# Attention and a low-rank mixer MLP on one core: the mixer by rows of tokens, turned by DMA, with a new order of score blocks and a new pacing

## The chip, the core and the metric

The kernel runs on one NeuronCore of a Trainium2 chip. Its engines run at the same time, each through its own instruction queue in order: TensorE (PE in the profile, PEld its weight loads), VectorE (DVE), ScalarE (ACT), GpSimd (POOL) and SyncE (SP), which here only issues DMA transfers. The kernel's matmuls write to PSUM; the other operands lie in SBUF, 128 partitions wide. Engines wait for each other by semaphores.

The metric is the device time of one execution in microseconds. The time before is 633.39 us, the median of three runs (633.01 to 634.63). A profile is one more execution, recorded by the hardware.

## The reference

Attention over 8 batches, 12 heads, 448 tokens and 64 dimensions a head, with q and k normalised by their root mean square; its result, laid side by side over the heads, is x (448 tokens x 768). A mixer adds a low-rank mix over tokens to x, which gives u, and a two-layer MLP follows.

```python
q_n, k_n = rmsnorm(q, g_q), rmsnorm(k, g_k)
attn = softmax(1.0 / np.sqrt(D) * q_n @ k_n.T)      # per batch and head
x = attn @ v                                        # heads side by side: 448 x 768
h = x.T @ U @ V                                     # U: 448 x 32, V: 32 x 448
u = x + h.T
ch = np.maximum(u @ w_ch1, 0.0) @ w_ch2             # 768 -> 3072 -> 768
out = u + ch
```

## The kernel before

*Tiles.* PE computes in bf16. 448 tokens are three windows of 128 columns and a remainder of 64 (`NJ = 3`, `R = 64`). Weights `w1b` and `w2b` stay in SBUF. `uT` (768 rows as 6 blocks of 128 partitions, 512 columns) holds u turned, with dimensions on the partitions; `hT` holds the hidden layer, 24 blocks of 128 rows. Even batches use columns 64 to 511 of both, odd batches 0 to 447, so that the last 64 tokens of an even batch and the last 64 of the following odd one lie side by side, in columns 448 to 511 and 384 to 447, and go through the second layer as one window of 128.

*Attention* (list `att`) goes by pairs of heads (`pr`, six a batch, 48 in all); two pairs make a group (`gi`, 24 in all) whose q, k and v are loaded and normalised together. For a pair there are four `Sc`: matmuls of kz by qT, 128x448 each, two in blocks 0 to 2 (a double block) and one in block 3, and behind each an exp on ACT into `E` (L333). `sc` has two buffers, so PE can be two blocks ahead of ACT. Two `V` then multiply `E` by v and the ones beside it, 14 matmuls each, and DVE divides (L352, L353) and writes `x`, which is laid out by rows of tokens.

*A block of norms* prepares a group: `squares` on ACT, `sums` on DVE, then `scale_all` (rs on ACT, L130 and L131; the scalings and the copies of v on POOL), then the turn of q and k. For the first six groups (`DMA_FROM = 6`) the turn is done by PE (`T`, `turn`); from then on by `turn_dma`: four DMA transposes on SP (L301, L303), and right behind them in the same queue `load`, six transfers for the group two further on (L88, L95, L99). SP also issues the output (L422).

*The mixer and MLP* (list `mlp`) goes by batches. `mix_t` multiplies x by U (24 small matmuls, L366), `mix_tr` turns the small result (L373). `mix` then makes one block of 128 dimensions of `uT`: a matmul of the turned product by V (L381, 448 columns), and four matmuls by an identity that turn x and add it in the same PSUM bank (L383, L384); DVE copies the bank to `uT` (L385). Six `mix` make a batch. `up` (24 a batch) is six matmuls of 448 columns, each reading all tokens of the batch from `uT`, and a relu on ACT. `down` goes by windows of 128 tokens and halves of 384 output dimensions, in four quarters of six matmuls (L404); the last quarter adds u with three identity matmuls that read `uT` (L410), DVE copies the bank to `ob` (L415) and, after the second half, two transfers take it out.

*PSUM.* `sc` has a pool of two buffers of its own (`ps_sc`). All other tiles (pv, ph, po, pt, pu, pw) share the four buffers of the pool `ps`, a bank each.

*The order of the work* is written out by hand. Before the first mixer, the six pairs of batch 0 run alone. Then a planner takes from `att` and `mlp` in turn, by the costs written beside each piece: the next attention piece is taken as long as attention's share done is not above the MLP's share, where the MLP's total is lessened by `LEAD` = 1.9 batches, so that attention is through before the MLP. Within `att`, a pair's order is Sc 0, V half 0 of the pair before, Sc 1, Sc 2, V half 1, Sc 3; the norms of the next group stand behind Sc 1 of every first pair of a group.

## Time and profile before

| | |
|---|---|
| median of three runs | 633.39 us |
| profiled execution, its own time | 632.76 us |
| its span, first to last instruction | 631.0 us |
| mean granted clock of TensorE | 0.993 |
| busy PE, ACT, DVE, POOL | 599.9, 317.3, 197.0, 139.2 us |
| MLP matmuls L391 and L404, busy | 239.5 and 240.5 us |
| first `mix_t` | at 47.77 us |
| end of the last matmul | about 626 us |

A line of the profile names the source line, the engine, the operation, the tiles written and read (`out<-in`), the shapes and how often; then busy time, mean time of one in ns, and the engine's idle time just before it with what ended it. A "q" behind an engine's name is its instruction queue, where DMA transfers are issued. PE's durations overlap, since matmuls are pipelined; what one costs is read from start to start.

### The profile page before, as it was taken

How to read it: one execution, taken by the hardware profiler on the slowest of the kernel's cores; microseconds unless marked ns; L12 is line 12 of the kernel's file. 1: busy time of each engine (PE TensorE's matmuls, PEld its weight loads, DVE VectorE, ACT ScalarE, POOL GpSimd, SP SyncE). 2: the span in 40 equal slices, each digit the busy share in tenths (PEclk: the TensorE clock that was granted, in tenths of full speed). 3: DMA queues.
4: the chain of work that ended last, by engine and by line, in shares of the span. 5: the costliest groups of instructions: out<-in, count | busy, mean ns of one | idle time of the engine just before them, and what ended most of it. 6: DMA issues, size and time to landing. Idle time of an engine off the chain costs nothing.

```text
span 631.0 us, 11686 instructions
## 1 busy us (share of the span) xinstructions
PE 599.9 (95%) x4880; PEld 363.2 (58%) x4880; DVE 197.0 (31%) x459; ACT 317.3 (50%) x483; POOL 139.2 (22%) x255
## 2 busy tenths in 40 slices
PE   3769999899999999989999999999999999999996
PEld 1545566555666556655566655665566655665564
DVE  7675233521334223242133422333223330130011
ACT  5785753377544674347644477337853344004300
POOL 4682203303302321330330332033033000000000
PEclk9989999999999999989999999999999999999999
DMA  9999944454366336526445623654425110120022
GB/s 260 243 240 238 239 100 88 119 133 97 66 153 148 84 89 151 124 68 125 109 79 153 155 46 95 150 118 92 107 45 79 42 26 1 25 51 1 1 51 50
DMA packets 95012, 66.88 MB, mean 106 GB/s; under 512 B 60528, under 2 KB 91376, under 8 KB 94960
## 3 DMA queue, kind: packets, MB, share of 16 engines
q1 hardware_dynamic: 88112, 56.22, 38.0%
q0 software_dynamic: 6576, 9.47, 8.2%
q8 instruction: 38, 0.62, 0.4%
q10 hardware_dynamic: 272, 0.46, 0.2%
q14 instruction: 14, 0.11, 0.1%
HBM read 52.19 MB, written 11.01 MB: 100 GB/s over the span
## 4 chain that ended last, share of the span: by engine, by line
PE 88%; DVE 5%; ACT 3%; issue 2%; POOL 1%; DMA 1%; POOLq 0%; DVEq 0%
PE po L404 35%; PE ph L391 34%; PE sc L332 9%; PE pv L349 5%; DVE uT L385 3%; ACT E L333 2%; PE po L410 1%; PE pv L345 1%; DVE ssq L124 1%; PE pt L282 1%; DMA qf<-in_q_dram 1%; ACT sq L121 1%; PE pu L366 1%; POOL kp L134 1%; PE ph L381 0%
## 5 line engine op out<-in xcount | busy, mean ns | idle before, releaser
L333 ACT ACTIVATE E<-sc,gg 128x896 bf16<-128x896 f32 x192 | 172.7, 910 | 140.7 <-PE sc L332 140.2
L391 PE MATMUL ph<-uT,w1b 128*128 128x448 bf16 x1152 | 239.5, 354 | 3.3 <-DVE uT L385 3.0
L404 PE MATMUL po<-w2b,hT 128*128 128x384 bf16 x1344 | 240.5, 326 | 0.0
L404 PEld LDWEIGHTS <-hT 128*128 128x128 bf16 x1344 | 127.7, 98 | 82.2
L391 PEld LDWEIGHTS <-w1b 128*128 128x128 bf16 x1152 | 110.0, 98 | 101.1 <-issue 5.7
L393 ACT ACTIVATE hT<-ph 128x448 bf16<-128x448 f32 x192 | 103.5, 544 | 126.6 <-PE ph L391 124.2
L332 PE MATMUL sc<-qT,kz 128*128 128x448 bf16 x336 | 95.9, 364 | 9.1 <-ACT E L333 8.3
L152 POOL TENSOR_TENSOR qn<-qf,rs 128x384 bf16<-128x384 f32 x36 | 29.9, 831 | 305.2 <-ACT rs L131 305.2
L415 DVE COPY ob<-po 128x384 f32<-128x384 f32 x56 | 31.2, 558 | 165.0 <-PE po L410 162.3
L352 DVE RECIPROCAL r<-pv 128x4 f32<-128x4 f32 x96 | 17.5, 182 | 207.8 <-PE pv L349 207.7
L349 PE MATMUL pv<-va,E 128*128 128x65 bf16 x1152 | 59.0, 196 | 0.8 <-ACT E L333 0.8
L349 PEld LDWEIGHTS <-E 128*128 128x128 bf16 x1152 | 52.2, 99 | 8.1 <-issue 1.1
L332 PEld LDWEIGHTS <-kz 128*128 128x128 bf16 x336 | 31.0, 99 | 33.1 <-issue 13.5
L124 DVE TENSOR_REDUCE ssq<-sq 128x14 f32<-128x896 f32 x48 | 49.7, 1076 | 1.1 <-ACT sq L121 1.1
L345 PE MATMUL pv<-vl,E 128*128 128x130 bf16 x192 | 42.9, 223 | 0.0
L353 DVE TENSOR_TENSOR x<-pv,r 128x256 bf16<-128x256 f32 x96 | 40.8, 424 | 3.3
L152 POOL TENSOR_TENSOR kp<-kf,rs 128x384 bf16<-128x384 f32 x36 | 29.9, 829 | 0.0
L385 DVE CAST uT<-ph 128x448 bf16<-128x448 f32 x48 | 26.6, 616 | 0.9 <-PE ph L384 0.7
L121 ACT ACTIVATE sq<-qf 128x896 f32<-128x896 f32 x24 | 22.6, 942 | 2.9 <-DMA qf<-in_q_dram 2.9
L345 PEld LDWEIGHTS <-E 128*128 128x128 bf16 x192 | 19.1, 99 | 7.1 <-issue 0.9
L121 ACT ACTIVATE sq<-kf 128x896 f32<-128x896 f32 x24 | 22.6, 940 | 0.0
L160 POOL CAST va<-vf 128x768 bf16<-128x768 f32 x24 | 20.4, 850 | 0.1
(67 smaller groups left out, 248.7 us busy)
## 6 DMA issues: line engine op xcount, KB each, us to landing
qf<-in_q_dram SPq DMA_DIRECT2D x24, 448.0 KB, 4.3
out_dram<-ob SPq DMA_DIRECT2D x56, 192.0 KB, 2.8
kf<-in_k_dram SPq DMA_DIRECT2D x23, 448.0 KB, 5.4
vf<-in_v_dram SPq DMA_DIRECT2D x48, 192.0 KB, 5.6
w1b<-in_moe_w_ch_dram POOLq DMA_DIRECT2D x4, 1152.0 KB, 20.9
w2b<-in_moe_w_ch_dram POOLq DMA_DIRECT2D x4, 1152.0 KB, 32.4
vf<-in_v_dram SPq DMA_DIRECT2D x48, 32.0 KB, 5.1
qT<-qn SPq DMA_TRANSPOSE x36, 3.0
```

The costliest lines, as they stand in the source:

```text
L121: nc.scalar.activation(sq, staged[gi][i], AF.Square)
L124: nc.vector.tensor_reduce(ssqs[gi][:, i, :], sqs.pop((gi, i)), AX, ALU.add)
L152: nc.gpsimd.tensor_tensor(main.rearrange("p (t i) d -> p i t d", i=2), src[:, c, :2 * NJ].rearrange("p (i t) d -> p i t d", i=2), rs[:, c, ...
L332: nc.tensor.matmul(sc[:, i, :S], kz[:, c:c + P], qT, start=True, stop=True)
L333: nc.scalar.activation(es[(b, pr)][:, 2 * r:2 * r + n, :], sc[:, :n, :S], AF.Exp, scale=scal, bias=bias)
L345: nc.tensor.matmul(pv[:, i].rearrange("p e d -> p (e d)"), E[:, NJ, w:w + P], vl[:, lp, :], start=True, stop=False)
L349: nc.tensor.matmul(pv[:, i, e, :], E[:, e * (NJ + 1) + j, w:w + P], va[:, (lp + 2 * e) * NJ + j, :], start=False, stop=(e == 1 and j == NJ ...
L353: nc.vector.tensor_tensor(xs[b].rearrange("p i (h d) -> p i h d", d=D)[:, 2 * half:2 * half + 2, h0:h0 + 3:2, :], pv[:, :, :, :D], r.rearr ...
L385: nc.vector.tensor_copy(uT[:, dt, off:off + S], ph)
L391: nc.tensor.matmul(ph, w1b[:, dt, ht * P:(ht + 1) * P], uT[:, dt, off:off + S], start=(dt == 0), stop=(dt == KD - 1))
L393: nc.scalar.activation(hT[:, ht, off:off + S], ph, AF.Relu)
L404: nc.tensor.matmul(po, hT[:, ht, col:col + P], w2b[:, ht, half * HALF:(half + 1) * HALF], start=(ht == 0), stop=False)
```

## The change

1. *Mixer by rows.* From batch 1 on (`ROWS_FROM = 1`) `mix` is gone. `mix_rows` works on one window of 128 tokens and 384 dimensions: three matmuls with V's columns as weights, and DVE adds the result to x in place (for the last 64 tokens, into a tile `u_rest`). After the second half one DMA transpose on SP takes the window into `uT`: 28 of them, four a batch, three of 128x768 and one of 64x768. Batch 0 keeps `mix` for `uT` and runs `mix_rows` between its `up`s, for the output alone.
2. *The output.* `down` has no identity matmuls; DVE adds u (from the x tile or `u_rest`) to the bank in place of the copy.
3. *Where it stands.* `mix_t`, `mix_tr` and the eight `mix_rows` of the next batch stand among the last 14 quarters of `down` of the batch before (`PRE = 14`); the last `mix_rows` has five quarters behind it.
4. *Tokens of odd batches* are ordered so that their remainder comes first (`WIN`, `POS_ODD`, the scaling before the turn), and U and V have a second form of their last window: one more transfer to `Ub`, 64 more columns in `Vm`.
5. *Attention's order.* Sc 0, Sc 1, V half 0 of the pair before, Sc 2, Sc 3, V half 1. Norms stand behind Sc 2 (behind Sc 1 for the very first pair). A batch's last two `V` stand together, ahead of the next batch's first block.
6. *Pacing.* `LEAD` is 1.8, and a function `due` spreads batch 1's attention over what the MLP does before `mix_t` of batch 1, and the rest over the rest.
7. *Buffers.* Three for x (two before), two for `ob` (three before). The small tiles of the gains live in an `ob` buffer. `prep_v` (the copies of V on POOL) moves from behind T of group 2 to behind the scaling of group 1.

```diff
-LEAD = 1.9
+ROWS_FROM = 1
+LEAD = 1.8
...
-    WIN = [0, P, 2 * P, S - P]
+    WIN = [[0, P, 2 * P, S - P], [R, R + P, R + 2 * P, 0]]
...
-    xp = ctx.enter_context(tc.tile_pool(name="xp", bufs=2))
-    outp = ctx.enter_context(tc.tile_pool(name="outp", bufs=3))
+    xp = ctx.enter_context(tc.tile_pool(name="xp", bufs=3))
+    outp = ctx.enter_context(tc.tile_pool(name="outp", bufs=2))
...
+    nc.gpsimd.dma_start(Ub[0:R, NJ + 1, :], Urows[:, 2 * NJ, :])
...
+    POS_ODD = [x + 1 for x in POS[:2 * NJ]] + [0]
...
+    u_rest = consts.tile([P, dm], BF16)
+
+    def urows(b, col, half):
+        h = slice(half * HALF, (half + 1) * HALF)
+        return u_rest[:, h] if col == SM else xs[b][:, (col - (0 if b % 2 else R)) // P, h]
+
+    def mix_rows(b, w, half):
+
+        odd = b % 2
+        off = 0 if odd else 64
+        h = slice(half * HALF, (half + 1) * HALF)
+        ph = ps.tile([P, HALF], FP32, name="pm", tag="ps")
+        vc = w * P if w < NJ else (SM if odd else S - P)
+        for i in range(HALF // P):
+            dt = half * (HALF // P) + i
+            nc.tensor.matmul(ph[:, i * P:(i + 1) * P], Vm[:, dt % NQ, vc:vc + P], tTs[b][:, dt // NQ, :],
+                             start=True, stop=True)
+        x = xs[b][:, w, h]
+        lo, hi = (0, P) if w < NJ else (0, R) if odd else (R, P)
+        dst = x if w < NJ else u_rest[lo:hi, h]
+        nc.vector.tensor_tensor(dst, ph[lo:hi], x[lo:hi], ALU.add)
+        if half == 1 and b >= ROWS_FROM:
+            full = xs[b][:, w, :] if w < NJ else u_rest[lo:hi, :]
+            c = off + w * P
+            nc.sync.dma_start_transpose(uT[:, :, c:c + hi - lo], full)
...
-        nd = HALF // P
-        for i in range(nd):
-            nc.tensor.matmul(po[:, i * P:(i + 1) * P], uT[:, half * nd + i, col:col + P], ident,
-                             start=False, stop=(i == nd - 1))
...
-        nc.vector.tensor_copy(ob[:, half * HALF:(half + 1) * HALF], po)
+        nc.vector.tensor_tensor(ob[:, half * HALF:(half + 1) * HALF], po, urows(b, col, half), ALU.add)
...
+    def norms(gi):
+        add_att(0.0, scale_all, gi)
+        if gi >= DMA_FROM:
+            add_att(0.0, turn_dma, gi)
+        if gi + 2 < len(groups):
+            add_att(0.0, load, gi + 2)
...
+        if pr == 0 and i > 0:
+            add_att(0.55, V, *pairs[i - 1], 0)
+            add_att(0.55, V, *pairs[i - 1], 1)
         add_att(0.38, Sc, b, pr, 0)
-        if i > 0:
-            add_att(0.55, V, *pairs[i - 1], 0)
...
         add_att(0.38, Sc, b, pr, 1)
...
+        if pr != 0:
+            add_att(0.55, V, *pairs[i - 1], 0)
...
+        if i == 0:
+            norms(gi + 1)
+        add_att(0.38, Sc, b, pr, 2)
+        if i > 0 and a == 0 and more:
+            norms(gi + 1)
...
+        add_att(0.19, Sc, b, pr, 3)
+        if pr != 0:
+            add_att(0.55, V, *pairs[i - 1], 1)
...
+    PRE = 14
...
+            if b < ROWS_FROM and ht % 2 == 0 and ht < 4 * NW:
+                mlp.append((0.17, mix_rows, (b, ht // 4, ht // 2 % 2), b))
...
+        if ROWS_FROM <= nb < B:
+            pre[n - PRE] = [(0.77, mix_t, (nb,), nb)]
+            pre[n - PRE + 1] = [(0.11, mix_tr, (nb,), nb)]
+            for w in range(NW):
+                for half in range(2):
+                    pre[n - PRE + 2 + 2 * w + half] = [(0.17, mix_rows, (nb, w, half), nb)]
...
+    m_end = m_all * (1.0 - LEAD / B)
+
+    def due(c):
+
+        if c < m_one:
+            return a_one * c / m_one
+        return a_one + (a_all - a_one) * (c - m_one) / (m_end - m_one)
+
...
-        take_att = ia < len(att) and (not may_mlp or ca / a_rest <= cm / m_rest)
+        take_att = ia < len(att) and (not may_mlp or ca <= due(cm))
...
-            if f is T and a == (2, 0):
-                prep_v()
+                if a == (1,):
+                    prep_v()
```

More of the change, by code (lines that the diff above doesn't have):

```diff
@@ L47 @@
     R = S - SM
-    WIN = [0, P, 2 * P, S - P]
-    NW = len(WIN)
+    WIN = [[0, P, 2 * P, S - P], [R, R + P, R + 2 * P, 0]]
+    NW = len(WIN[0])
     D1 = D + 1
@@ L147, in scale_dma @@
                 dst = normed[gi][0][:, :, c]
-                main, rest = dst[:, :2 * NJ], dst[:, 2 * NJ]
+                odd = groups[gi][0] % 2
+                main, rest = dst[:, odd:odd + 2 * NJ], dst[:, (1 - odd) * 2 * NJ]
             else:
@@ L189 @@
     make_identity(nc, ident)
-    grow = consts.tile([1, 2, D], FP32)
+    small = outp.tile([P, dm], FP32, name="ob", tag="ob")
+    grow = small[0:1, 0:2 * D].rearrange("o (i d) -> o i d", i=2)
     for i, g in enumerate((g_q, g_k)):
@@ L206 @@
     bias = gg[:, 1:2]
-    gp = consts.tile([1, 2 * D + 1], FP32)
-    ones = consts.tile([1, P], FP32)
+    gp = small[0:1, 2 * D:4 * D + 1]
+    ones = small[0:1, 4 * D + 1:4 * D + 1 + P]
     nc.vector.memset(ones, 1.0)
@@ L243, in load_w2 @@
         )
-    Ub = consts.tile([P, NW, rank], BF16)
-    nc.vector.memset(Ub[:, NJ, :], 0.0)
+    Ub = consts.tile([P, NJ + 2, rank], BF16)
+    nc.vector.memset(Ub[:, NJ:, :], 0.0)
     Urows = moe_U.rearrange("(p j) r -> p j r", j=NT)
@@ L251 @@
     nc.gpsimd.dma_start(Ub[R:P, NJ, :], Urows[:, 2 * NJ, :])
+    nc.gpsimd.dma_start(Ub[0:R, NJ + 1, :], Urows[:, 2 * NJ, :])
     NQ = P // rank
     Vf = outp.tile([P, dm], FP32, name="ob", tag="ob")[:, :S]
-    Vm = consts.tile([P, NQ, S], BF16)
+    Vm = consts.tile([P, NQ, S + R], BF16)
     for m in range(NQ):
@@ L265, in prep_v @@
                                   cols[:, :2 * NJ].rearrange("r (i t) p -> r i t p", i=2))
-            nc.gpsimd.tensor_copy(Vm[r, m, SM:], cols[:, 2 * NJ])
+            nc.gpsimd.tensor_copy(Vm[r, m, SM:S], cols[:, 2 * NJ])
     tb_bufs = [consts.tile([P, 2 * P], BF16, name=f"tb{i}") for i in range(2)]
@@ L280, in turn @@
         pt = pts[(gi, i)] = ps.tile([P, NT, 2, R], BF16, name="pt", tag="ps")
+        pos = POS_ODD if i == 0 and groups[gi][0] % 2 else POS
         for j in range(NT):
-            nc.tensor.transpose(pt[:, POS[j]].rearrange("p a r -> p (a r)"),
+            nc.tensor.transpose(pt[:, pos[j]].rearrange("p a r -> p (a r)"),
                                 normed[gi][i][:, j].rearrange("p c d -> p (c d)"), ident)
@@ L343, in V @@
         for i in range(2):
-            w = WIN[2 * half + i]
+            w = WIN[b % 2][2 * half + i]
             nc.tensor.matmul(pv[:, i].rearrange("p e d -> p (e d)"), E[:, NJ, w:w + P], vl[:, lp, :],
@@ L365, in mix_t @@
             for j in range(NW):
-                nc.tensor.matmul(pt[:, dt, :], xs[b][:, j, dt * P:(dt + 1) * P], Ub[:, j, :],
+                nc.tensor.matmul(pt[:, dt, :], xs[b][:, j, dt * P:(dt + 1) * P], Ub[:, j if j < NJ else NJ + b % 2, :],
                                  start=(j == 0), stop=(j == NW - 1))
@@ L380, in mix @@
         xb = xs[b][:, :, dt * P:(dt + 1) * P]
-        nc.tensor.matmul(ph, tTs[b][:, dt // NQ, :], Vm[:, dt % NQ, :], start=True, stop=False)
+        nc.tensor.matmul(ph, tTs[b][:, dt // NQ, :], Vm[:, dt % NQ, :S], start=True, stop=False)
         for j in range(NJ):
@@ L404, in down @@
             nc.tensor.matmul(po, hT[:, ht, col:col + P], w2b[:, ht, half * HALF:(half + 1) * HALF],
-                             start=(ht == 0), stop=False)
+                             start=(ht == 0), stop=(ht == KH - 1))
         if part < nparts - 1:
             return
-        nd = HALF // P
-        for i in range(nd):
-            nc.tensor.matmul(po[:, i * P:(i + 1) * P], uT[:, half * nd + i, col:col + P], ident,
-                             start=False, stop=(i == nd - 1))
         if half == 0:
@@ L434 @@
         more = gi + 1 < len(groups)
+        if pr == 0 and i > 0:
+            add_att(0.55, V, *pairs[i - 1], 0)
+            add_att(0.55, V, *pairs[i - 1], 1)
         add_att(0.38, Sc, b, pr, 0)
-        if i > 0:
-            add_att(0.55, V, *pairs[i - 1], 0)
-        if a == 1 and more:
-            add_att(0.39 if gi + 1 < DMA_FROM else 0.0, T, gi + 1, 0)
         if a == 0 and i > 0 and more:
@@ L443 @@
         add_att(0.38, Sc, b, pr, 1)
-        if a == 0 and more:
-            add_att(0.0, scale_all, gi + 1)
-            if gi + 1 >= DMA_FROM:
-                add_att(0.0, turn_dma, gi + 1)
-            if gi + 3 < len(groups):
-                add_att(0.0, load, gi + 3)
+        if pr != 0:
+            add_att(0.55, V, *pairs[i - 1], 0)
+        if a == 1 and more:
+            add_att(0.39 if gi + 1 < DMA_FROM else 0.0, T, gi + 1, 0)
+        if i == 0:
[3 more added lines that the diff above has]
+            norms(gi + 1)
         if a == 1 and more:
             add_att(0.39 if gi + 1 < DMA_FROM else 0.0, T, gi + 1, 1)
-        add_att(0.38, Sc, b, pr, 2)
-        if i > 0:
+        add_att(0.19, Sc, b, pr, 3)
+        if pr != 0:
             add_att(0.55, V, *pairs[i - 1], 1)
-        add_att(0.19, Sc, b, pr, 3)
         if a == 1 and gi + 2 < len(groups):
@@ L466 @@
             done_at[a[0]] = n + 1
+    PRE = 14
     mlp = []
     for b in range(B):
-        if b == 0:
-            mlp.append((0.77, mix_t, (b,), b))
-            mlp.append((0.11, mix_tr, (b,), b))
-        for dt in range(KD):
-            mlp.append((0.39, mix, (b, dt), b))
+        if b < ROWS_FROM:
+            if b == 0:
+                mlp.append((0.77, mix_t, (b,), b))
+                mlp.append((0.11, mix_tr, (b,), b))
+            for dt in range(KD):
+                mlp.append((0.39, mix, (b, dt), b))
         for ht in range(KH):
             mlp.append((1.14, up, (b, ht), b))
+            if b < ROWS_FROM and ht % 2 == 0 and ht < 4 * NW:
+                mlp.append((0.17, mix_rows, (b, ht // 4, ht // 2 % 2), b))
         cols = (64, 192, 320) if b % 2 == 0 else (384, 0, 128, 256)
-        for col in cols:
+        n = len(cols) * 8
+        nb = b + 1
+        pre = {}
+        if ROWS_FROM <= nb < B:
[4 more added lines that the diff above has]
+                    pre[n - PRE + 2 + 2 * w + half] = [(0.17, mix_rows, (nb, w, half), nb)]
+        for c, col in enumerate(cols):
             for half in range(2):
                 for part in range(4):
-                    last = col == cols[-1] and half == 1
-                    if b + 1 < B and last and part == 1:
-                        mlp.append((0.77, mix_t, (b + 1,), b + 1))
-                    if b + 1 < B and last and part == 3:
-                        mlp.append((0.11, mix_tr, (b + 1,), b + 1))
-                    mlp.append((0.98 + (0.17 if part == 3 else 0.0), down, (b, col, half, part, 4), b))
+                    mlp.extend(pre.get(c * 8 + half * 4 + part, []))
+                    mlp.append((0.98, down, (b, col, half, part, 4), b))
     todo = [(load_w1, (c, 4)) for c in range(4)] + [(load_w2, (c, 4)) for c in range(4)]
@@ L519 @@
     a_from = done_at[0]
-    a_rest = sum(c for c, _, _ in att[a_from:])
-    m_batch = sum(m[0] for m in mlp if m[3] == 0)
-    m_rest = sum(m[0] for m in mlp) - LEAD * m_batch
+    a_all = sum(c for c, _, _ in att[a_from:])
+    a_one = sum(c for c, _, _ in att[a_from:done_at[1]])
+    m_all = sum(m[0] for m in mlp)
+    m_one = 0.0
+    for m in mlp:
+        if m[3] > 0:
+            break
+        m_one += m[0]
+    m_end = m_all * (1.0 - LEAD / B)
[3 more added lines that the diff above has]
+        return a_one + (a_all - a_one) * (c - m_one) / (m_end - m_one)
     while ia < len(att) or im < len(mlp):
         may_mlp = im < len(mlp) and ia >= done_at[mlp[im][3]]
-        take_att = ia < len(att) and (not may_mlp or ca / a_rest <= cm / m_rest)
+        take_att = ia < len(att) and (not may_mlp or ca <= due(cm))
         if take_att:
```

## The prediction, made before the changed kernel ran

> **What bounds the kernel now.** I read the page first: busy shares, the chain that ended last, the groups. Then the PE timeline for the price of each piece, the waits for where PE stands still, and the queue of SP, because the change puts new transfers into it.

> ```profile
> PE 599.9 (95%) x4880; PEld 363.2 (58%) x4880; DVE 197.0 (31%) x459; ACT 317.3 (50%) x483; POOL 139.2 (22%) x255
> PE 88%; DVE 5%; ACT 3%; issue 2%; POOL 1%; DMA 1%; POOLq 0%; DVEq 0%
> L385 DVE CAST uT<-ph 128x448 bf16<-128x448 f32 x48 | 26.6, 616 | 0.9 <-PE ph L384 0.7
> qT<-qn SPq DMA_TRANSPOSE x36, 3.0
> kz<-kp SPq DMA_TRANSPOSE x36, 3.5
> ```

> PE is the bound: 88% of the chain. A microsecond of matmul removed, or of PE idle added, is a microsecond of span. The last two rows price a transfer of the kind that the change adds: issue to landing 3.0 us (448 packets of 256 B) and 3.5 us (896).

> PE timeline, start and duration, two pieces of `mix` and the end of the last `down`:

> ```profile
> 121.96 0.35 PE L381 MATMUL ph<-Vm,tT 128*128 128x448 bf16 x1
> ...
> 122.34 0.35 PE L381 MATMUL ph<-Vm,tT 128*128 128x448 bf16 x1
> ...
> 621.57 0.33 PE L410 MATMUL po<-ident,uT 128*128 128x128 bf16 x3
> ...
> 621.74 4.06 PE L404 MATMUL po<-w2b,hT 128*128 128x384 bf16 x24
> 625.64 0.33 PE L410 MATMUL po<-ident,uT 128*128 128x128 bf16 x3
> ```

> One `mix` costs PE 0.385 us (start to start), three 128x128 matmuls 0.17, a quarter of a `down` 0.976 (621.74 to 625.64, by 4), an `up` 1.14, a double score block 0.38, a single one 0.19, a `V` 0.50.

> The queue of SP around one block of norms (four turns of q and k, six loads), and the copy whose output transfer stands behind it in program order:

> ```profile
> 120.94 1.25 SPq L301 DMA_TRANSPOSE qT<-qn  x1
> 123.02 1.24 SPq L303 DMA_TRANSPOSE kz<-kp  x1
> 124.35 1.58 SPq L301 DMA_TRANSPOSE qT<-qn  x1
> 125.98 1.30 SPq L303 DMA_TRANSPOSE kz<-kp  x1
> 127.37 0.91 SPq L88 DMA_DIRECT2D qf<-in_q_dram  x1
> 128.38 0.43 SPq L88 DMA_DIRECT2D kf<-in_k_dram  x1
> 128.86 1.39 SPq L95 DMA_DIRECT2D vf<-in_v_dram  x2
> 130.30 1.95 SPq L99 DMA_DIRECT2D vf<-in_v_dram  x2
> 132.35 1.19 SPq L422 DMA_DIRECT2D out_dram<-ob  x2
> ```

> ```profile
> 122.16 0.56 DVE L415 COPY ob<-po 128x384 f32<-128x384 f32 x1 [0.85 <-PE po L410]
> ```

> `ob` was ready at 122.72, its transfer was issued at 132.35. SP goes in order, so whatever stands behind a block waits for all of it, 9.6 us here. Nobody needs an output soon, so before the change this costs nothing. That row decides my forecast.

> **The change, part by part** (profiled execution: span 631.0, own time 632.76, 0.63 under the median of 633.39).

> *Removed from PE.* 42 `mix` (batches 1 to 7) x 0.385 = 16.2. Identity matmuls of 56 `down` x 0.17 = 9.5. *Added:* 64 `mix_rows`, three 128x128 matmuls each, the form of L410: 64 x 0.17 = 10.9. Net -14.8.

> *The wait for uT at a batch's start.* The waits give PE 3.0 us in 7 waits on uT plus 5.7 us of PEld "issue" at L391. From batch 1 on, the gaps in the PE timeline there, beyond a matmul's 0.19, come to 0.55, 2.4, 0.25, 0.6 and 0.65, and the clock fell to half behind the second (below, 1.7): 6.1 in all. I take -5.5 and leave 0.6 for the handover at the clean starts.

> *The start, to 47.77 us (the first `mix_t`).* ACT sets it. Two double blocks first keep ACT fed past `V` and `T`: ACT waited 8.0 us for scores between 9 and 53 us. The four Vm casts (POOL 33.5 to 38.1, which held the third scaling back to 38.16 although its rs ended at 36.97) move to POOL's idle time 22.2 to 27.1. The first mixer no longer has three score blocks and a pair of squares ahead of it. I worked the ACT chain through by rows (0.91 a double block, 0.6 a single, 1.7 the squares) and get the first `mix_t` near 43.3, with 0.9 us less PE work done. Gain 0 to 4.5; I take 3, below the 3.6, as the weights land no earlier.

> *At nothing:* DVE gets 64 adds and loses 42 casts (0.55 each): about +10 us on an engine 31% busy; uncovered, only the last add, under 0.1. One more Ub transfer, 0.54 us on POOL, ahead of a 2.0 us wait. Windows, POS_ODD and WIN: same instructions. Third x buffer: it only lets `V` run further ahead. Two `ob` buffers for three: 0 to +3, taken 0; an output has twelve quarters, some 12 us and the attention between them, until its buffer is wanted, and needs a block's hold to miss that (rival B). LEAD and the pacing change which matmuls follow which, not their number; in the planner's list no batch's attention has to be forced ahead of a waiting mixer, the tightest being `mix_t` of batch 1, one quarter (0.976) behind its last `V`, whose reciprocal and multiply take 0.6.

> Without lateness: 632.8 - 14.8 - 5.5 - 3 = **609.5**.

> *Moved onto SP.* Four turns of u per batch, 28 in all (SP issue 1.25 each, between q and kz in size; landing 3.0 to 3.5). The first `up` of a batch waits on all four, since each of its matmuls reads 448 columns. The built program's order on SP shows where they stand. Batch 2, for one:

> ```
> uT<-x x2, out x2, uT<-x, [q/k turns x4, loads x6 of group 13], uT<-u_rest
> ```

> A block stands between the first and the second turn at batch 1, between the third and the fourth at batches 2 and 3, and ahead of all four at batches 4 and 5. Batches 6 and 7 are clean.

> How long a block holds SP: it waits for rs on ACT, then for POOL's scaling. rs to the first turn is 2.85, the first turn to the last load's end 10.5 to 11.4. From the start of the exp that rs stands behind to the end of the loads, blocks inside a `down` stretch took 14.2 to 15.3, mostly 14.3; elsewhere up to 16.7. PE to exp adds 0.26. So SP is free 14.6 us after the score block that precedes the norms. Behind loads a transfer landed 3.8 to 5.3 after issue (median 4.2), otherwise about 3.0.

> Cover is what PE does from that score block's end to the first `up`, from the planner's list at the prices above:

> - batch 1: cover 16.3; free 14.6 + turn, out x2, turn (4.0) + landing 3.0 = 21.6; late **5.3**
> - batch 2: cover 7.6; 14.6 + 4.2 = 18.8; late **11.2**
> - batch 3: cover 9.1; 18.8; late **9.7**
> - batch 4: cover 19.4; 14.6 + 5.3 + 3.0 = 22.9; late **3.5**
> - batch 5: cover 20.3; 22.9; late **2.6**

> Together 32.3. Bounds: 14.2 and a landing of 3.8 give 28; 16.5 and 5.3 give 45. Turns as dear as the longest existing issue (2.1) would add about 8 more.

> *The clock behind a stall.* Windows view, columns width, busy of each engine, granted clock, DMA share, GB/s; just after a 2.3 us gap in PE:

> ```profile
> 277.85:281.26 3.41, 3.41 (x22) 1.89 (x21) 0.41 (x2) 2.04 (x5) 2.65 (x5) 0.50 0.00 0
> 281.26:285.00 3.74, 3.74 (x21) 1.96 (x20) 0.20 (x1) 2.16 (x4) 2.85 (x7) 1.00 0.42 70
> ```

> PE at half speed for 3.41 us: 1.7 us lost. Five stalls x 1.7 = 8.5, bounds 0 (gaps of 1.7 us at 25.7 and 117 had no such stretch) and 17 (two stretches each). [...]

> Sum: 609.5 + 32.3 + 8.5 = 650.3 for such an execution, **651** against the median.

> **Rivals.**
> *A. The turns are hidden: faster.* If a block held SP under about 11 us instead of 14.3, lateness would be about 8, 6 and 2, less than the 23 gained. At no lateness it gives 610. For it: POOL is 22% busy, and a turn itself lands in 3 us against 4.9 us of `down` left behind the last one. Against it: no block with loads was shorter than 14.2, and the output at 132.35 shows the hold. [...] Here the transfer takes 3 us and the wait for the sequencer 9.6.

> *B. The hold is as said, but what it holds spreads.* Outputs behind a block keep one of two `ob` buffers, DVE's add waits, po and pv keep their banks, PE stands. Before, DVE waited 2.6 us on a transfer ahead of one copy (113.5) with three buffers. Nine outputs on SP stand right behind a block; at 1.5 us each, with holds at their slow end (+5), about 669.

> *C. Only half of the lateness counts,* because ACT reaches rs earlier or loads issue faster: 16 + 5 gives 631, about no change.

> **How the numbers follow.** Forecast 0.64 (639 to 663), B 0.19 (663 to 680), C 0.09 (624 to 639), A 0.08 (609 to 624). Range 636 to 670: it leaves out A, the lower part of C and the tail of B, just under 2 in 10. Within 0.3% (1.9 us, about what a measurement of this kernel can tell from no change) only part of C falls: 0.02. Faster: A and part of C, 0.10. Slower: 0.88.

> **What would show it.** PE's waits at the `up` line name the DMA of uT, five large ones, the two largest at batches 2 and 3, none above 1 us at batches 6 and 7. SP's timeline shows the turn of u_rest right behind the last load of a block, over 10 us after its add. The page counts 186 matmuls fewer (378 removed, 192 added). The granted clock shows half-speed stretches behind the stalls. The first `mix_t` starts before 46. The forecast is wrong if `up` never waits over 3 us on a transfer, or if the largest wait names ACT or DVE.

## The result: 652.1 us, and the profile after

The changed kernel took 652.1 us (median, 651.1 to 652.5) against 633.2 us before (median of four executions, 630.9 to 634.6): a ratio of 1.030 with a 95% interval of 1.027 to 1.033. It is slower by 18.9 us; 651 had been forecast. The profiled execution took 651.12 us, with a span of 649.3.

The page of the changed kernel: busy time of each engine, the granted clock in 40 slices, the chain that ended last, and two groups (busy, mean ns, idle time before them); the last line is the group of `up` in the kernel before.

```profile
PE 592.8 (91%) x4694; PEld 355.2 (55%) x4694; DVE 206.9 (32%) x481; ACT 319.0 (49%) x483; POOL 139.2 (21%) x256
...
PEclk9889999999999699996999989999999999999999
...
PE 86%; DMA 6%; DVE 3%; SPq 2%; issue 1%; ACT 1%; POOL 0%; DVEq 0%
...
L427 PE MATMUL ph<-uT,w1b 128*128 128x448 bf16 x1152 | 244.5, 360 | 33.0 <-DMA vf<-in_v_dram 20.4
...
L447 DVE TENSOR_TENSOR ob<-po,x 128x384 f32<-128x384 f32 x48 | 26.7, 557 | 91.2 <-PE po L440 91.0
```

```profile
L391 PE MATMUL ph<-uT,w1b 128*128 128x448 bf16 x1152 | 239.5, 354 | 3.3 <-DVE uT L385 3.0
```

PE has 186 matmuls fewer and is busy 7 us less, yet its share fell from 95% to 91%: it now stands still. Transfers, 1% of the chain before, are 6%, with 2% of SP's queue behind them. (That share alone does not show the loss: it is 6% too in the kernel of experiment two in which no turn is late.) One group holds nearly all the new idle time, the matmuls of `up` (L427), 33.0 us where it was 3.3. The add that produces `ob` (L447) waited for PE alone, 91.0 of 91.2 us.

What PE waited for from 42 us on (us in total, times, longest):

```profile
PE ph L427 <- DMA vf<-in_v_dram: 20.4, 2, 10.9
PE ph L427 <- DMA uT<-u_rest: 12.6, 3, 5.1
PE pw L382 <- DVE tb L377: 2.0, 2, 1.6
```

There are five waits at L427, all at the first `up` of a batch. Two of them name a load of v, which `up` does not read. The loads had landed by 217.92 at batch 2; the turn landed at 218.18, and PE went on 0.09 us later. The queue of SP at batch 2 shows what PE needed (start, time of the issue, operation):

```profile
200.47 1.28 SPq L421 DMA_TRANSPOSE uT<-x  x1
203.50 1.19 SPq L310 DMA_TRANSPOSE qT<-qn  x1
...
208.51 1.30 SPq L312 DMA_TRANSPOSE kz<-kp  x1
209.90 0.87 SPq L91 DMA_DIRECT2D qf<-in_q_dram  x1
...
211.35 1.39 SPq L98 DMA_DIRECT2D vf<-in_v_dram  x2
212.78 1.26 SPq L102 DMA_DIRECT2D vf<-in_v_dram  x2
214.14 1.22 SPq L421 DMA_TRANSPOSE uT<-u_rest  x1
```

The add whose result the last of these transfers turns, and PE on both sides of the wait:

```profile
201.25 0.56 DVE L417 TENSOR_TENSOR u_rest<-pm,x 64x384 bf16<-64x384 f32 x1 [0.77 <-PE pm L412]
```

```profile
206.19 1.14 PE L440 MATMUL po<-w2b,hT 128*128 128x384 bf16 x6
218.27 2.40 PE L427 MATMUL ph<-uT,w1b 128*128 128x448 bf16 x6 [10.94 <-DMA vf<-in_v_dram]
...
221.16 1.30 PE L427 MATMUL ph<-uT,w1b 128*128 128x448 bf16 x6
```

`u_rest` was ready at 201.81. Its turn was issued at 214.14, 12.3 us later, behind four turns of q and k and six loads, and landed 4.04 us after that. At batch 3 the same turn went out at 293.92 and landed at 297.95; PE resumed at 298.04.

Windows around that wait (width, busy time of each engine, granted clock, DMA share, GB/s):

```profile
207.30:218.27 10.97, 0.04 (x2) 0.03 (x2) 0.56 (x1) 0.10 (x1) 0.00 (x0) 0.65 0.93 214
218.27:220.91 2.64, 2.64 (x14) 1.29 (x15) 0.00 (x0) 0.21 (x1) 0.00 (x0) 0.50 0.04 10
220.91:224.00 3.09, 3.09 (x27) 1.72 (x25) 0.97 (x3) 1.78 (x3) 0.00 (x0) 1.00 0.00 0
```

Behind the stall PE works 2.64 us at half speed: the six matmuls of one `up` take 2.40 us there, and 1.30 once the clock is full again.

### The profile page after: what moved, and what is told of

Read it like the earlier page. It is cut to its first block, busy times and chain, and to the rows that moved or that the text cites. A ratio compares the mean times of both kernels' runs of the same rounds, so it can differ in the third digit from the quotient of the medians.

```text
span 649.3 us, 11405 instructions
## 1 busy us (share of the span) xinstructions
PE 592.8 (91%) x4694; PEld 355.2 (55%) x4694; DVE 206.9 (32%) x481; ACT 319.0 (49%) x483; POOL 139.2 (21%) x256
## 4 chain that ended last, share of the span: by engine, by line
PE 86%; DMA 6%; DVE 3%; SPq 2%; issue 1%; ACT 1%; POOL 0%; DVEq 0%
PE ph L427 35%; PE po L440 33%; PE sc L341 9%; PE pv L358 5%; DMA vf<-in_v_dram 2%; DMA kf<-in_k_dram 2%; PE pm L412 2%; PE pv L354 1%; DMA uT<-u_rest 1%; DVE ssq L127 1%; DMA qf<-in_q_dram 1%; PE pt L291 1%; PE pu L375 1%; SPq L421 1%; SPq L91 0%
## 5 line engine op out<-in xcount | busy, mean ns | idle before, releaser
L427 PE MATMUL ph<-uT,w1b 128*128 128x448 bf16 x1152 | 244.5, 360 | 33.0 <-DMA vf<-in_v_dram 20.4
L427 PEld LDWEIGHTS <-w1b 128*128 128x128 bf16 x1152 | 111.1, 99 | 134.5 <-issue 21.4
L341 PE MATMUL sc<-qT,kz 128*128 128x448 bf16 x336 | 98.4, 367 | 6.1 <-ACT E L342 5.3
L447 DVE TENSOR_TENSOR ob<-po,x 128x384 f32<-128x384 f32 x48 | 26.7, 557 | 91.2 <-PE po L440 91.0
L127 DVE TENSOR_REDUCE ssq<-sq 128x14 f32<-128x896 f32 x48 | 49.7, 1077 | 11.8 <-ACT sq L124 11.8
L341 PEld LDWEIGHTS <-kz 128*128 128x128 bf16 x336 | 32.9, 100 | 31.9 <-issue 7.6
L417 DVE TENSOR_TENSOR x<-pm,x 128x384 bf16<-128x384 f32 x48 | 26.5, 553 | 15.6 <-PE pm L412 15.5
L412 PE MATMUL pm<-tT,Vm 128*128 128x128 bf16 x192 | 21.1, 219 | 0.0
```

What stands on the lines that cost most here:

```text
L127: nc.vector.tensor_reduce(ssqs[gi][:, i, :], sqs.pop((gi, i)), AX, ALU.add)
L341: nc.tensor.matmul(sc[:, i, :S], kz[:, c:c + P], qT, start=True, stop=True)
L412: nc.tensor.matmul(ph[:, i * P:(i + 1) * P], Vm[:, dt % NQ, vc:vc + P], tTs[b][:, dt // NQ, :], start=True, stop=True)
L427: nc.tensor.matmul(ph, w1b[:, dt, ht * P:(ht + 1) * P], uT[:, dt, off:off + S], start=(dt == 0), stop=(dt == KD - 1))
```

## The experiments

The rival theories of the roughly 42 us between the forecast without lateness (609.5) and the time measured were: the place of the turns in SP's order; the turns themselves, as transfers that take DMA time or land slowly; outputs held behind a block (rival B); and something in the new order of the attention. In the tables a gap is the time from the start of PE's last matmul to the start of the first `up`; a matmul's own 0.17 us is in it. Medians of the kernel before were 632.7, 632.3 and 633.0 us on the chips that these runs used. The third buffer of x, the two of `ob`, the order of the tokens and the pacing were not run singly; they are in every kernel below but that of experiment four.

**One: the block of norms behind the last turn.** Where a block of q/k turns and loads would be issued between a batch's third and fourth turn, it is issued behind the fourth. That happens at batches 2 and 3.

```diff
             c, f, a = att[ia]
-            f(*a)
+            if left == 1 and f in (turn_dma, load):
+                held.append((f, a))
+            else:
+                f(*a)
...
+            if f is mix_t and a[0] >= ROWS_FROM:
+                left = NW
+            if f is mix_rows and a[0] >= ROWS_FROM and a[2] == 1:
+                left -= 1
+                if left == 0:
+                    for g, b in held:
+                        g(*b)
+                    held = []
```

> The changed kernel, with one thing moved: where a block of norms would be put on SP between the third and the fourth turn of u (batches 2 and 3), its turns of q and k and its loads are put behind the fourth. Same transfers, same matmuls. Theory (SP held in order by the block): the waits at the first up of batches 2 and 3 (11.1 and 9.5 us in the trace) go to 0, with the half-speed stretches behind them (1.3 and 2.4 us); those of batches 1, 4 and 5 stay at 5.3, 4.4 and 3.3. 652.1 - 24.3 = 628, faster than before the change. Rival (the turn itself is slow, or the DMA engines are full): the fourth turn lands no earlier for being issued earlier, 648 to 652.

Measured: 628.3 us, ratio 0.993 (0.990 to 0.995), as expected. The queue of SP at batch 2 in this kernel, and what PE waited for from 50 us on:

```profile
199.62 1.29 SPq L421 DMA_TRANSPOSE uT<-x  x1
201.11 1.18 SPq L421 DMA_TRANSPOSE uT<-u_rest  x1
202.78 1.19 SPq L310 DMA_TRANSPOSE qT<-qn  x1
```

```profile
PE ph L427 <- DMA uT<-u_rest: 12.0, 3, 4.8
```

The two longest waits are gone; those of batches 1, 4 and 5 stayed (gaps 5.1, 4.2 and 3.5 us). The same transfers, in another order at two places, are worth 23.8 us and turn the loss into a small gain.

**Two: the turns earlier.** `PRE` says how many quarters of `down` before a batch's end the mixer of the next batch begins. Nothing else is changed by hand; the planner's list follows it, since the attention of batch 1 is spread over what stands ahead of that batch's mixer.

```diff
-    PRE = 14
+    PRE = 16     # and 18, 20, 24
```

> PRE 16 in place of 14: the mixer of the next batch stands two quarters of down earlier. Theory: the same sum of cover and hold, from the planner's list of this kernel, gives waits of 3.2, 0, 9.6, 2.9, 1.9, 0, 0 at batches 1 to 7, 17.6 together against 33.6 measured with 14; the block of batch 2 now falls behind the fourth turn, that of batch 3 does not. With one or two half-speed stretches less: 632 to 635. Rival (the turns are just 3 to 11 us too slow, wherever they stand): two quarters more cover, some 2.7 us, off each of five waits, 13 together, and batch 2 still waits 8: 637 to 640.

> PRE 20: six quarters earlier. Theory: by the planner's list no wait is left at any of the seven batches; 652.1 - 33.6 - 8.7 = 609.8, 608 to 613. Rival (slow turns): about 8 us off each wait: batch 2 keeps 3, batch 3 some 1.5, 614 to 618. Rival (what stands beside the turns costs: two ob buffers, the pacing): above 620.

| `PRE` | us (median) | ratio to before (95%) | gaps at the first `up` of batches 1 to 5 |
|---|---|---|---|
| 14 | 652.1 | 1.030 (1.027 to 1.033) | 5.4, 11.3, 9.7, 4.6, 3.5 |
| 16 | 632.1 | 1.000 (0.998 to 1.002) | 3.5, none, 9.5, 3.7, 2.2 |
| 18 | 611.6 | 0.966 (0.965 to 0.968) | none over 1.0 |
| 20 | 607.1 | 0.961 (0.959 to 0.963) | none |
| 24 | 611.0 | 0.965 (0.964 to 0.967) | none |

At 16 the waits, less 0.17 each, are 3.3, 0, 9.3, 3.5 and 2.0 us. Expected were 3.2, 0, 9.6, 2.9 and 1.9: which block falls behind which turn was read from the program's order alone. At 20 the version beats both kernels, by 0.9 us more than the expected range allowed. Its queue of SP at batch 2 and, below, PE at the first `up`:

```profile
170.72 1.92 SPq L310 DMA_TRANSPOSE qT<-qn  x1
...
180.00 1.26 SPq L102 DMA_DIRECT2D vf<-in_v_dram  x2
181.37 1.25 SPq L421 DMA_TRANSPOSE uT<-x  x1
182.72 1.17 SPq L454 DMA_DIRECT2D out_dram<-ob  x2
183.98 3.14 SPq L421 DMA_TRANSPOSE uT<-x  x2
187.37 1.18 SPq L421 DMA_TRANSPOSE uT<-u_rest  x1
```

```profile
200.29 2.43 PE L427 MATMUL ph<-uT,w1b 128*128 128x448 bf16 x12
```

Here a block stands ahead of all the turns, and they still go out 13 us before `up` starts: the hold is the same (10.5 us from the first turn of q to the end of the last load, at batch 2 of either kernel), its cover is not. Its page, and the longest of its waits from 50 us on:

```profile
PE 580.6 (96%) x4694; PEld 350.6 (58%) x4694; DVE 207.8 (34%) x481; ACT 318.6 (53%) x483; POOL 139.1 (23%) x256
...
L427 PE MATMUL ph<-uT,w1b 128*128 128x448 bf16 x1152 | 237.1, 352 | 0.2 <-DVE uT L394 0.2
```

```profile
PE pw L382 <- DVE tb L377: 0.5, 1, 0.5
```

The idle time before L427 fell from 33.0 to 0.2 us, and PE's busy time from 592.8 to 580.6: the one trace has eight half-speed stretches ahead of its end, the other none. The turns are all there and take 2.3 to 5.6 us to land, in the changed kernel 2.4 to 5.3. So it is not their duration that costs.

**Three: the turns left out.**

```diff
+        nc.vector.memset(uT[:, :, 0:64], 0.0)
...
-        if half == 1 and b >= ROWS_FROM:
+        if False:
```

The output is thus no longer that of the reference.

> The changed kernel without the 28 turns of u: batches 1 to 7 go on with what batch 0 left in uT (the text may say: its output is not the reference's); the mixer's matmuls, adds and outputs stay. Theory: all that is left out is the wait, 609 to 613, the same as PRE 20. Rival (other parts of the change hold the kernel up): clearly above 615.

Measured: 609.0 us, ratio 0.964 (0.961 to 0.967). `up` waits for nothing. With the turns in and the same `PRE`, but hardly late, it is 610.0 (experiment seven, with one wait of 1.2 us left), a ratio of 0.964 too: no cost of the 28 turns on SP and on the DMA engines shows in these two.

**Four: the order of the attention alone.** The kernel before, with the new order of scores, values and norms and the early casts of Vm, but the old mixer, the old pacing and the old output.

```diff
+        if pr == 0 and i > 0:
+            add_att(0.55, V, *pairs[i - 1], 0)
+            add_att(0.55, V, *pairs[i - 1], 1)
         add_att(0.38, Sc, b, pr, 0)
-        if i > 0:
-            add_att(0.55, V, *pairs[i - 1], 0)
...
-            if f is T and a == (2, 0):
-                prep_v()
+                if a == (1,):
+                    prep_v()
```

> The kernel before with the new order of attention alone: two double blocks first, norms behind the third block, a batch's last two V together, prep_v behind the scaling of group 1. Mixer, planner and LEAD as before. Theory: the gain at the start, about 2 to 3 us, and nothing else: 630 to 631. Rival (the order matters only while ACT is alone, and the work it leaves behind is done later): 633.

Measured: 629.0 us, ratio 0.995 (0.994 to 0.997), a gain of 3.4 us where 2 to 3 had been expected. The first `mix_t` starts at 43.52 us (before 47.77, changed kernel 43.13). What ACT waited for between 9 and 53 us, the row that speaks on the reason:

```profile
ACT E L333 <- PE sc L332: 7.9, 9, 2.7
```

Before it was 8.0. So the gain at the start is real, but ACT is not kept better fed by the two double blocks. The mixer starts earlier because less stands ahead of it: PE runs 44 score matmuls before the first `mix_t` and ACT 24 exps, in the kernel before 49 and 26. From 629.0 to the 607.1 of `PRE` 20 is 21.8 us, which is what the mixer by rows with its pacing is worth when no turn is late; 14.8 and 5.5 had been summed.

**Five: a longer block.** Every load from group 9 on is issued twice, which lengthens SP's hold and adds nothing else but its traffic.

```diff
+        if gi >= 9:
+            for i in range(2):
+                load_qk(gi, i)
+            load_v(gi)
```

> The changed kernel with the six loads of every block from group 7 on issued twice (groups 9 and up; the second copy rewrites the same bytes). Theory: SP is held 5 to 6 us longer at each of the five late batches: waits of about 10.5, 16.5, 15, 9.5 and 8.5 us, 676 to 682. Rival (the time is in the turn or in POOL's scaling): within 3 us of 652.

Measured: 689.2 us, ratio 1.090 (1.087 to 1.093), 7 to 13 us more than expected. The queue of SP ahead of the same turn at batch 2, and two of PE's waits:

```profile
223.30 1.26 SPq L102 DMA_DIRECT2D vf<-in_v_dram  x2
...
228.40 1.26 SPq L102 DMA_DIRECT2D vf<-in_v_dram  x2
229.70 1.28 SPq L425 DMA_TRANSPOSE uT<-u_rest  x1
```

```profile
PE ph L431 <- DMA vf<-in_v_dram: 37.7, 2, 19.2
...
PE pm L416 <- DVE ob L451: 3.9, 1, 3.9
```

The gaps at the five `up` grew to 11.8, 18.8, 19.4, 4.4 and 8.4 us. Less 0.17 each they are 62.0, near the 60 expected; beyond that, half-speed stretches lose 14.7 us behind the stalls where the changed kernel loses 8.7, and the last line is a new wait. What DVE did there:

```profile
390.44 0.56 DVE L451 TENSOR_TENSOR ob<-po,x 128x384 f32<-128x384 f32 x1 [5.55 <-DMA out_dram<-ob]
```

This is rival B's mechanism: an output behind the longer block keeps an `ob` buffer, DVE's add waits 5.55 us, and PE stands for 3.9. In the changed kernel DVE shows no such wait.

**Six: PE kept busy through the stalls.** Ahead of the first `up` of batches 1 to 5 PE gets 24, 52, 44, 18 and 12 matmuls whose result nobody reads. The turns are as late as they were; only the clock behind the stalls changes.

```diff
+WARM = {1: 24, 2: 52, 3: 44, 4: 18, 5: 12}
...
+        if ht == 0 and b in WARM:
+            pd = ps.tile([P, S], FP32, name="pd", tag="ps")
+            for i in range(WARM[b]):
+                nc.tensor.matmul(pd, w1b[:, i % KD, :P], w1b[:, i % KD, :S], start=True, stop=True)
```

> The changed kernel with 24, 52, 44, 18 and 12 extra matmuls of 448 columns (4.5, 9.8, 8.3, 3.4 and 2.3 us of PE) ahead of the first up of batches 1 to 5, into a bank that nobody reads. They end before the turns land, so the waits end when they did, but PE is busy until then. Theory (half-speed stretches cost 8.7 us behind the stalls): 643 to 645. Rival (the clock has no part, the loss is all wait): 652.

Measured: 643.7 us, ratio 1.019 (1.017 to 1.021), 8.4 us under the changed kernel. PE at batch 2 and the window behind it:

```profile
206.00 10.00 PE L429 MATMUL pd<-w1b 128*128 128x448 bf16 x52
216.91 0.35 PE L432 MATMUL ph<-uT,w1b 128*128 128x448 bf16 x1 [0.91 <-DMA vf<-in_v_dram]
```

```profile
216.91:220.91 4.00, 4.00 (x33) 2.34 (x34) 0.97 (x3) 1.59 (x3) 0.00 (x0) 1.00 0.06 13
```

The first `up` starts with a granted clock of 1.00. The 8.4 us are the price of the half-speed stretches behind the stalls; 8.5 had been put into the sum, and those stretches of the changed kernel, read one by one, lose 1.7, 1.3, 2.4, 1.6 and 1.7, together 8.7. (The two kernels ran on different chips; by their ratios to the kernel before, the difference is 6.9 us, with some 2.5 either way.)

**Seven: the loads behind the turns, with `PRE` as it is.** As in experiment one, but the loads of any block that falls among the turns of a batch wait until the fourth turn is issued.

```diff
-            if left == 1 and f in (turn_dma, load):
+            if left == 1 and f is turn_dma or left > 0 and f is load:
```

> The changed kernel (PRE 14) with the order on SP alone mended: from the mixer's start to the fourth turn of u, the six loads of a block wait until the fourth turn is issued; at batches 2 and 3 its turns of q and k too. Theory: the loads are 5 us of the hold; without them the five waits are 0.5, 0, 0, 0, 0, and the time is that of PRE 20, 607 to 612. Rival (the hold is POOL's scaling, which still stands ahead of the turns at batches 1, 4 and 5): waits of some 5, 4 and 3 us stay there, 625 to 630 as in the run that moved the block at batches 2 and 3 alone.

Measured: 610.0 us, ratio 0.964 (0.962 to 0.966). One gap is left, 1.3 us at batch 1. At batches 4 and 5, where POOL's scaling still stands ahead of the turns, no wait is left: without the loads the hold is short enough there. The order of SP's queue can thus be mended at its issue as well as by an earlier mixer.

**Eight: where the best `PRE` lies.**

> PRE 18. By the planner's list waits of 0, 0, 0, 0.5 and 0.5 are left: 607 to 610, no half-speed stretch behind them. Rival (a lead of six quarters is what it takes): one of the large waits stays, above 612.

> PRE 24: the next batch's mixer right behind the last up, or eight quarters behind it in odd batches. Theory: nothing is left to gain over 20, 606 to 608. Rival (an earlier mixer asks for its batch's attention earlier, and ACT cannot follow): 610 or more.

Both missed: 611.6 at 18 is 1.6 us above the expected range, 611.0 at 24 is 3.0 above it and has the price of the rival. At 18 the turns are in time, but the matmuls of `mix_rows` wait for the copies that they read. Its waits from 50 us on:

```profile
PE pm L412 <- DVE tT L384: 3.0, 2, 1.6
PE ph L427 <- DMA uT<-u_rest: 0.8, 2, 0.6
```

With a third of 0.2 they come to 4.0 us, against 0.9 at 20: 3.1 of the 4.5 us between the two kernels. At 24 such waits are small (2.2 us in all), none of them for ACT, so the rival's reason is not seen; PE stands idle 3.1 us longer in that trace than in the one at 20, before 52 us and behind it in about equal parts, and what brings it is open. DVE waits 4.0 and 3.6 us there for an output's transfer, as in rival B, without PE standing for it. The clock does not account for it. The traces of 18 and 24 show two half-speed stretches of 3.4 us between 35 and 50 us, that of 20 none; but the other executions of 18, with a mean granted clock of 0.998 in place of 0.993, took 611.3 to 611.8, and those of 24, with 0.996 and 0.997 in place of 0.992, took 610.9 to 611.2.

## Why the prediction was right

The direction, the size and the place were right; the working held step by step, but for the terms named below.

- **The five waits.** Predicted 5.3, 11.2, 9.7, 3.5 and 2.6, together 32.3. Measured, gaps less 0.17: 5.3, 11.1, 9.5, 4.4 and 3.3, together 33.6. Batches 6 and 7 have none. The two terms that were short are those where a block stands ahead of all four turns.
- **A turn right behind loads.** Predicted to land 4.2 us after its issue, measured 4.04 and 4.03 at batches 2 and 3.
- **The clock.** Predicted 8.5, measured 8.7 in the trace and 8.4 by experiment six. That all five stalls pay was right. The two shortest came out longer than I had them, 4.4 and 3.3 us against 3.5 and 2.6, so of the stalls here none was as short as the 2.3 us gap of the kernel before, which a half-speed stretch followed too (277.85).
- **The sum without lateness, 609.5.** Measured: 651.1 less 33.6, 8.7 and a new wait of 1.8 leaves 607.0, and the kernel in which no turn is late, at `PRE` 20, takes 607.1. The mixer by rows was undervalued by about 1.5 us (21.8 against 20.3), the start by some 0.4 to 0.6.
- **A wait that the sum lacks.** PE stands 1.8 us for `tb`, a cast on DVE (it starts no matmul from 268.19 to 270.12, of which 0.17 is a matmul's own; "PE pw", 1.6 us of idle time, in the waits). DVE was not short of time, as the term for its added work had it; it stood, in order, for a turn of q ahead of the cast. The timeline of DVE (in brackets the idle time before, and what ended it):

```profile
269.35 0.45 DVE L317 TENSOR_SCALAR qT<-qT,gg 128x896 bf16<-128x896 bf16 x1 [4.22 <-DMA qT<-qn]
269.71 0.35 DVE L377 CAST tb<-pu 128x192 bf16<-128x192 f32 x1
```

  The same order as on SP, on another engine: I had asked what stands behind the blocks on SP, and not what stands on DVE behind the scaling of `qT`. With the turns of u left out this wait stays (1.6), so they do not cause it. It made the sum 1.8 too low, the term above 2.4 too high; so the total came out within 1 us, 650.3 predicted and 651.1 measured for the profiled execution. That these two, and the 1.3 by which the waits were short, nearly cancel is luck; the waits and the clock came out by the mechanism.
- **The start.** 3 taken, 3.4 measured by experiment four; the first `mix_t` at 43.1 was predicted near 43.3. The reason that I gave first, ACT fed past `V` and `T`, is wrong: its wait for scores stayed (7.9 us against 8.0).
- **Rival A** had the right price, 610: it is reached by 609.0, 610.0 and 607.1 as soon as the turns are not late. Its condition is false here: the turn of batch 2, which takes 1.2 us to issue and 4.0 to land, lost 12.3 us behind other entries of the same queue.
- **Rival B** did not come: PE stood for an output only with the loads doubled. **Rival C** is out, since the waits came at full size.
- **One mark was misnamed.** I had said that PE's waits would name the DMA of uT. The two largest name a load of v. The landing 0.09 us ahead of PE, not the name, tells what released it, and experiment one confirms it.

## What to carry to other kernels

A transfer that an engine needs soon should not be queued behind a block that waits for other engines. Here SP issued its entries in the program's order, so the turn of batch 2 went out 12.3 us after its data was ready, and it was this lateness, at five batches, not the 4.0 us that the transfer took, which cost 33.6 us of PE. Whether such a move pays can be worked out before it runs (the five waits came to 32.3 us so, and to 33.6 when measured), by writing down the program's order on the queue and setting, for each entry, the time when the block ahead is done against the work that the consumer still has. When a change loses for this reason, move the transfer (or its producer) earlier, or the block later: here a mixer four quarters earlier or more, or the loads behind the turns, turned +3.0% into -3.4% or better, with no change to the computation.

## What the runs showed of the hardware that was not expected

Two gaps of nearly the same length differ in what follows them. The first windows are of the kernel before, where a gap (1.9 us without a matmul running) lies wholly in one window; the second of the `PRE` 16 kernel, where a gap of 1.8 us begins 0.5 us ahead of the window (columns as above):

```profile
274.42:277.84 3.42, 1.31 (x7) 0.48 (x5) 2.62 (x4) 0.37 (x1) 0.00 (x0) 1.00 0.00 0
277.84:281.25 3.41, 3.41 (x22) 1.90 (x21) 0.40 (x2) 2.05 (x5) 2.64 (x5) 0.50 0.00 0
```

```profile
433.89:437.30 3.41, 2.09 (x12) 1.12 (x13) 0.07 (x1) 0.76 (x2) 0.00 (x0) 1.00 0.62 149
437.30:440.72 3.42, 3.42 (x31) 2.04 (x30) 0.61 (x2) 2.73 (x6) 1.53 (x3) 1.00 0.00 0
```

PE was busy 1.31 of 3.42 us in the one, and the next window ran at 0.50; 2.09 of 3.41 in the other, and the next ran at 1.00. Near the start (26 to 47 us) the changed kernel has three stretches, the kernel before one and that with `PRE` 20 (mean clock 0.999) none, and executions of one kernel differ as well. There the stretches cost nothing that these runs can tell: with the turns left out, an execution with a mean clock of 1.000 took 609.4 us and three with 0.993 or 0.994 took 608.6 to 609.7; in experiment seven two with 0.999 took 610.2, and two with 0.993 took 609.6 and 609.9. In the traces of these two kernels all stretches ahead of the end lie before 50 us.
